# Two attention blocks on one core: row maxima and weighted values turned by VectorE

## The chip, the cores and the metric

The kernel runs on one core of a Trainium2 chip. Times are device microseconds of that core. The engines of the core are named as the profile names them: PE is TensorE's matrix product and PEld its weight load, DVE is VectorE, ACT is ScalarE, POOL is GpSimd and SP is SyncE, which here only issues transfers (DMA). Each engine works its own queue in order. A profile is one execution with every instruction's start and length; the times that are compared are those of several executions without it.

## The reference

Two attention blocks A and B read the same input `x` of 2048 rows and 640 features; a gate mixes their results. Each has 32 heads of 20 features.

```python
qkv = (x @ wqkv).reshape(B, S, 3, H, Dh).transpose(2, 0, 3, 1, 4)
scores = einsum("bhqd,bhkd->bhqk", q, k) * Dh ** -0.5
o = einsum("bhqk,bhkd->bhqd", softmax(scores), v)
attn = o.transpose(0, 2, 1, 3).reshape(B, S, D) @ wo
g = sigmoid((x * gate_w).sum(-1, keepdims=True))
return g * attn_A + (1 - g) * attn_B
```

All inputs and the output are float32. Nothing is masked, so every head has a full 2048 x 2048 matrix of scores.

## The kernel before, in words

The heads are taken four at a time (`GH`), which gives 8 groups for each block and 16 in all. The queries are taken in four blocks of 512 (`QB`). A group with a query block is a unit; there are 64 units. A unit is worked in 8 steps, each with two key tiles of 128 keys, so the main loop has 512 steps.

Each score is computed twice. The first time, in `max_mm`, queries stand on the partitions and 512 keys along the row; only the row's maximum is wanted. Most of these tiles are reduced by VectorE straight from PSUM (line 587). For some, two tiles are combined first: ScalarE keeps the positive part of a difference (line 580) and VectorE adds and takes the maximum in one instruction (line 584). These maxima run up to 15 steps (`LEAD`) ahead of their use. The second time, in `scores`, keys stand on the partitions and 512 queries along the row (line 639). The negated maximum of each query is already in the product, because four extra rows of the query tile `QT` (60 to 63 in each half of 64 partitions) hold it, split into float16 pieces, against rows of a constant in the key tile. ScalarE then takes the exponential out of PSUM (line 642), and `values` multiplies it with the values (line 657). The values have a 21st column of ones, so that each head's 32 rows of the PSUM tile `acc` hold 20 rows of weighted values, then in row 20 (`DH`) the sum of the weights.

Float32 operands of the projections are split into two float16 parts, "high" and "low", and three products are added up. The weighted values are split in the same way before they are stored for the output projection.

Two places are of interest here.

`finish_max` runs when a unit's maxima are complete. `mneg` has 128 queries on the partitions and 16 columns: 4 heads by 4 query tiles. It has to become rows of `QT`, with queries along the row. After a pause, TensorE transposes it (line 600), ScalarE copies and scales the 16x128 result (line 605), GpSimd makes four float16 pieces of it (lines 608 and 610), one transfer writes them to DRAM (line 613), and four transfers read them into `QT` (line 617).

`take_acc` runs when a unit's values are complete. ScalarE copies `acc` to SBUF (line 742), and so frees `acc` for the next unit, which has only this one tile. A transfer collects the four rows of sums as 128x16 (line 748), VectorE takes the reciprocal (line 750), GpSimd splits it into two float16 parts (lines 752 to 754), two transfers lay them out as 8 rows of 512 (line 758), and TensorE spreads these rows over the 32 rows of each head by a product with the constant `sel` (line 763). VectorE multiplies (line 765), GpSimd splits into high and low (lines 768 and 769), and transfers store them (line 774).

The order of all this is fixed while the program is built. A string per step says what comes after what: `e0` and `e1` are score products of the two halves of the partitions, `m0` and `m1` the products for maxima, `V` a values block of eight products, `X` a slot for a piece of a projection:

```python
STEP = ("e0 m1 V e1 m0 e0 m1 e1 m0 e0 m1 e1 m0 V e0 m1 e1 m0",
```

The two other strings have one and three slots `X`, and are taken when projections are due. `finish_max`, `take_acc` and the like are generators in the list `side`. Each `e` advances every one of them by one turn, so a step has 8 turns; `turns(n)` waits n of them. A generator that yields `PRODUCT` is parked until `product()` takes it on, directly ahead of the next `V`. PSUM has `acc` and seven other banks. `take()` picks the bank that a small model of the engines (`clock`, `free_at`, `spend`, `give`, `tick_block`) expects to be free first.

Of the kernel before, what the change touches and what calls it, by code (L numbers as in the profile page):

```python
# [10 lines left out]
F16 = mybir.dt.float16  # L11
F32 = mybir.dt.float32
I32 = mybir.dt.int32
AF = mybir.ActivationFunctionType
OP = mybir.AluOpType
AX = mybir.AxisListType
# [3 lines left out]
P = 128  # L20
# [3 lines left out]
DH = 20  # L24
NT = S // P
NC = D // P
GH = 4
NG = H // GH
GF = GH * DH
QB = 512  # L30
# [5 lines left out]
XE = 7  # L36
QKS = 2.0 ** -12
PARTS = (0, 176, 344, 512)
RS = 2.0 ** 13
OB = 3  # L40
OWAIT = 20
SUM0, SUM1 = -8, 1.9
# [10 lines left out]
T_SCORE, T_MODE, T_VALUES, T_READY = 0.217, 0.1, 0.85, 0.39  # L53
T_EXP, T_MAX, T_BACK = 0.478, 0.6, 0.15
REST = 6
PRODUCT = "product"
ORDER = (0, 2, 1, 3)
LOW = -3.0e38
MS = 2.0 ** 15
# [3 lines left out]
def kernel(  # L63
# [10 lines left out]
    nc = tc.nc  # L74
# [4 lines left out]
    consts = ctx.enter_context(tc.tile_pool(name="consts", bufs=1))  # L79
    wts = ctx.enter_context(tc.tile_pool(name="wts", bufs=2))  # L80
# [4 lines left out]
    ident = consts.tile([P, P], F32, name="ident")  # L85
    make_identity(nc, ident)
    ones = consts.tile([5, P], F32, name="ones")
    nc.vector.memset(ones, 1.0)
    head = consts.tile([2 * GH, GH], F32, name="head")
    nc.gpsimd.tensor_tensor(head, ident[:2 * GH, :GH], ident[:2 * GH, GH:2 * GH], op=OP.add)  # L90
    sel = consts.tile([2 * GH, GH, 32], F16, name="sel")
    nc.vector.tensor_scalar(sel, head.unsqueeze(2).to_broadcast([2 * GH, GH, 32]), 1.0 / RS, None, op0=OP.mult)
    xx = consts.tile([P, 2, NC, S], F16, name="xx")
    xh, xl = xx[:, 0], xx[:, 1]

# [6 lines left out]
    acc = psum.tile([P, QB], F32, name="acc")  # L102
# [15 lines left out]
    clock = {"pe": 0.0, "done": 0.0, "act": 0.0, "dve": 0.0}  # L118
    rows_free = [0.0, 0.0]
    block_end = [0.0, None]  # L120
    free_at, held = [0.0] * NB, set()
    now = [-1]

    def take():

        i = min((k for k in range(NB) if k not in held), key=lambda k: free_at[k])
        held.add(i)
        return i, banks[i]

    def spend(engine, cost, ready=0.0):  # L130

        clock[engine] = max(clock[engine], ready) + cost
        return clock[engine] + T_BACK

    def give(i, t):
        free_at[i] = t
        held.discard(i)
# [7 lines left out]
    def tick_block(cost, ready=0.0):  # L145

        begin = block_end[0] if now[0] < 0 and block_end[1] == rows_free else max(rows_free) + T_MODE
        clock["pe"] = max(begin, ready)
        rows_free[:] = [clock["pe"] + cost + T_MODE] * 2
        block_end[:] = [clock["pe"] + cost, list(rows_free)]  # L150
        clock["done"] = clock["pe"] + cost + T_READY - T_MODE
# [229 lines left out]
    def turns(n):  # L381

        for _ in range(n if now[0] >= 0 else 0):
            yield
# [162 lines left out]
    mparts, ready = {}, set()  # L547
# [42 lines left out]

    def finish_max(g, qb):

        mneg = wts.tile([P, 16], F32, name="mneg", tag="mneg", bufs=2)
        nc.vector.tensor_reduce(mneg, mparts.pop((g, qb)).rearrange("p a b c d -> p (a b c) d"), axis=AX.X,
                                op=OP.max, negate=True)
        for _ in range(REST):
            yield
        yield PRODUCT
        i, pt = take()
        nc.tensor.transpose(pt[:16, :P], mneg, ident)  # L600
        tick_block(0.1, free_at[i])
        yield
        give(i, spend("act", 0.3, clock["done"]))
        mt = wts.tile([16, P], F32, name="mt", tag="mt", bufs=2)
        nc.scalar.activation(mt, pt[:16, :P], AF.Copy, scale=0.5 / MS)  # L605
        m4 = wts.tile([16, 4, P], F16, name="m4r", tag="m4r", bufs=2)
        for k in range(2):
            nc.gpsimd.tensor_copy(m4[:, k, :], mt)  # L608
        for k in range(2):
            nc.gpsimd.tensor_tensor(m4[:, 2 + k, :], mt, m4[:, 0, :], op=OP.subtract)  # L610
        yield from turns(8)
        ms = m_scr[qb % 2]
        nc.sync.dma_start(ms.rearrange("k r q -> r k q"), m4)
        yield from turns(5)
        for h in range(GH):
            base, pair = 60 + 64 * (h % 2), h // 2
            nc.sync.dma_start(QT[g % 2][base:base + 4, pair, qb * QB:(qb + 1) * QB],
                              ms[:, 4 * h:4 * h + 4, :].rearrange("k t q -> k (t q)"))
        ready.add((g, qb))
# [118 lines left out]

    def take_acc(g, qb):

        ot = work.tile([P, QB], F32, name="ot", bufs=2)
        nc.scalar.activation(ot, acc, AF.Copy)  # L742
        spend("act", T_EXP)
        few, many = (2, 8) if g == 2 * NG - 1 else (6, 24)
        sq = work.tile([P, 16], F32, name="sq", bufs=2)
        sh = work.tile([P, 2, 16], F16, name="sh", bufs=2)
        yield from turns(few)
        nc.sync.dma_start(sq, ot.rearrange("(h e) q -> h e q", e=32)[:, DH, :])
        yield from turns(many)
        nc.vector.reciprocal(sq, sq)  # L750
        spend("dve", 0.25)
        nc.gpsimd.tensor_scalar(sq, sq, RS, None, op0=OP.mult)
        nc.gpsimd.tensor_copy(sh[:, 0], sq)
        nc.gpsimd.tensor_tensor(sh[:, 1], sq, sh[:, 0], op=OP.subtract)
        yield from turns(few)
        sr = work.tile([2 * GH, QB], F16, name="sr", bufs=1)
        for k in range(2):
            nc.sync.dma_start(sr[GH * k:GH * k + GH], sh[:, k])
        yield from turns(many)
        yield PRODUCT  # L760
        i, pt = take()
        tick_block(T_SCORE, free_at[i])
        nc.tensor.matmul(pt, sel.rearrange("k h e -> k (h e)"), sr, start=True, stop=True)  # L763
        yield
        nc.vector.tensor_tensor(ot, ot, pt, op=OP.mult)  # L765
        give(i, spend("dve", 0.7, clock["done"]))
        o = work.tile([P, 2, QB], F16, name="on", bufs=2)
        nc.gpsimd.tensor_copy(o[:, 0], ot)  # L768
        nc.gpsimd.tensor_tensor(o[:, 1], ot, o[:, 0], op=OP.subtract)
        if g < 2 * NG - 1:  # L770
            yield from turns(16)
            for h in range(GH):
                f = (g % NG * GH + h) * DH
                nc.sync.dma_start(o_scr[g // NG][:, f:f + DH, qb * QB:(qb + 1) * QB].rearrange("k d q -> d k q"),
                                  o[32 * h:32 * h + DH])
            stored.add((g, qb))
        else:
            last.append((qb, o))
# [9 lines left out]
    def take_last():  # L788

        ot = work.tile([P, QB], F32, name="ot", bufs=2)  # L790
        nc.scalar.activation(ot, acc, AF.Copy)
        i, pt = take()
        one = ident.rearrange("p (h e) -> p h e", e=32)[:, :, DH]
        for t in range(4):
            nc.tensor.matmul(pt[:, 4 * t:4 * t + 4], ot[:, t * P:(t + 1) * P], one, start=True, stop=True)
        rc = work.tile([P, 16], F32, name="sq", bufs=2)
        nc.vector.reciprocal(rc, pt[:, :16])
        give(i, spend("dve", 0.3))
        i, pt = take()
        nc.tensor.transpose(pt[:16, :P], rc, ident)  # L800
        rt = wts.tile([16, P], F32, name="mt", tag="mt", bufs=2)
        nc.scalar.activation(rt, pt[:16, :P], AF.Copy)
        give(i, spend("act", 0.3))
        i, pt = take()
        for t in range(4):
            nc.tensor.matmul(pt[:, t * P:(t + 1) * P], picks[0].rearrange("p k e -> p (k e)")[:, t * P:(t + 1) * P], rt,
                             start=True, stop=True)
        o = work.tile([P, 2, QB], F16, name="on", bufs=2)
        for t in range(4):
            c = slice(t * P, (t + 1) * P)  # L810
            nc.vector.tensor_tensor(ot[:, c], ot[:, c], pt[:, c], op=OP.mult)
            nc.scalar.activation(o[:, 0, c], ot[:, c], AF.Copy)
            nc.gpsimd.tensor_tensor(o[:, 1, c], ot[:, c], o[:, 0, c], op=OP.subtract)
        give(i, spend("dve", 1.2, spend("act", T_EXP)))
        return o
# [30 lines left out]
    start = start_stack.enter_context(tc.tile_pool(name="start", bufs=1))  # L846
# [53 lines left out]
    r, inv = found  # L900
# [4 lines left out]
    for f in drains:  # L905
# [7 lines left out]
                            op=OP.subtract)  # L913
# [70 lines left out]
    work = ctx.enter_context(tc.tile_pool(name="work", bufs=2))  # L984
# [17 lines left out]
    for g in range(2 * NG):  # L1002
        b = g * NQ * NS
        n = g + 1
        if n < 2 * NG:
# [3 lines left out]
            i = g // 4 + 1  # L1009
            if i < 4:  # L1010
                if g % 4 == 0:
                    z, c0 = i // 2, 320 * (i % 2)
                    parts = max_tasks([[(wqkv[z], part * D + c0 + 160 * k) for k in range(2)] for part in range(2)],
                                      lambda m, i=i: scales_qk(i, m))
# [6 lines left out]
            if gg < NG and g % 2 == 0:  # L1021
                load, scale, split = weights_v(gg)
# [4 lines left out]
    for z in range(2):  # L1027
        b = (6, 12)[z] * NQ * NS
        parts = max_tasks([[(wo[z], 160 * k) for k in range(4)]], lambda m, z=z: scales_o(z, m), wrow[z])
        tasks(b + 8, 1, parts)  # L1030
        b = ((NG - 1) * NQ * NS + 4, (NG + 5) * NQ * NS - 4)[z]
# [89 lines left out]
    for G in range(STEPS + 1):  # L1121
        g, qb, i = unit_of(G)
# [12 lines left out]
        for what in (STEP[blocks] if maxima or some else LATE + " X" * (blocks == 2)).split():  # L1135
            k = count[what] = count.get(what, 0) + 1
# [58 lines left out]
```

## Time and profile before

| what | value |
|---|---|
| median of 3 runs | 2867.42 us (2866.15 to 2869.01) |
| profiled execution | 2865.34 us, span 2863.5 us |
| granted TensorE clock | 0.997 |
| busy PE, ACT, DVE, POOL | 98%, 90%, 84%, 24% of the span |
| moved by DMA | 114.77 MB in 176761 packets |

The span runs from the first to the last instruction of the profile. "Busy" counts the time in which an engine had at least one instruction under way; register, semaphore and transfer-issuing instructions do not count. Products are pipelined, so several can be under way at once, and their modelled lengths overlap. The chain of waits is followed back from the last instruction: at each step to what released it, or to the instruction ahead of it on its engine; a line's share of the chain says how much of the span hung on it. In the groups of instructions, `out<-in` are the program's tile names, `x63` is the count, then come busy microseconds, the mean of one in nanoseconds, and the idle time of the engine just before them with what ended it. In the order of time, a row has its start, its length, the engine, the line, the operation, the tiles and the count of merged instructions.

### The profile page before, as it was taken

What the parts mean: (1) busy time and instruction counts of PE and PEld (TensorE: products, weight loads), DVE (VectorE), ACT (ScalarE), POOL (GpSimd) and SP (SyncE); (2) the same over time, 40 slices, a digit from 0 to 9 for tenths busy, and PEclk for the clock granted to TensorE, in tenths of its full rate; (3) what the DMA queues carried; (4) which work ended last, traced back from release to release, by engine and by line L of the source; (5) the groups of instructions that cost most, each with busy time, mean ns of one, the idle gap of its engine ahead of it and who ended that gap; (6) DMA issues with size and microseconds to landing.
All of it is one profiled execution on the core that took longest, in us unless ns stands there. A gap on an engine that the chain in (4) does not pass through costs nothing.

```text
span 2863.5 us, 63124 instructions
## 1 busy us (share of the span) xinstructions
PE 2805.2 (98%) x23489; PEld 982.2 (34%) x23489; DVE 2405.1 (84%) x4637; ACT 2567.4 (90%) x5249; POOL 678.5 (24%) x1103
## 2 busy tenths in 40 slices
PE   6999999999999999999999999999999999999998
PEld 3533223342323323343233333334433333332222
DVE  6688898878898898978988888887788888889982
ACT  3799999989999999989999999998899999888987
POOL 5322113221221212233431111322112233120011
PEclk9999999999999999999999999999999999999999
DMA  4110101001020101202022020210202112221222
GB/s 134 41 38 6 37 10 41 15 15 31 14 52 17 31 15 27 50 10 52 18 45 53 14 60 16 47 37 21 47 21 54 44 35 66 62 72 52 69 61 74
DMA packets 176761, 114.77 MB, mean 40 GB/s; under 512 B 111812, under 2 KB 150396, under 8 KB 176452
## 3 DMA queue, kind: packets, MB, share of 16 engines
q1 hardware_dynamic: 173908, 109.12, 15.9%
q8 instruction: 184, 3.01, 0.4%
q0 software_dynamic: 1600, 0.96, 0.2%
q14 instruction: 125, 1.02, 0.1%
q10 hardware_dynamic: 944, 0.66, 0.1%
HBM read 48.89 MB, written 26.61 MB: 26 GB/s over the span
## 4 chain that ended last, share of the span: by engine, by line
PE 91%; DVE 3%; ACT 2%; DMA 1%; issue 1%; POOL 1%; SPq 0%; POOLq 0%; ACTq 0%; DVEq 0%
PE acc L657 34%; PE bank L639 19%; PE bank L377 19%; PE bank L576 17%; DVE mpart L587 2%; ACT pt L642 1%; PE bank L763 1%; ACT rl L580 1%; PE bank L600 0%; DMA xs<-in_A_x_dram 0%; DMA wv<-in_A_wqkv_dram 0%; DVE rl L584 0%; PE bank L185 0%; ACT ot L742 0%; PE bank L880 0%
## 5 line engine op out<-in xcount | busy, mean ns | idle before, releaser
L642 ACT ACTIVATE pt<-bank 128x512 f32<-128x512 f32 x4096 | 2179.1, 613 | 154.5 <-PE bank L639 85.6
L587 DVE TENSOR_REDUCE mpart<-bank 128x1 f32<-128x512 f32 x2976 | 1883.8, 684 | 337.4 <-PE bank L576 202.8
L657 PE MATMUL acc<-pt,v 128*21 128x512 f32 x8192 | 1081.8, 600 | 2.5 <-ACT ot L742 2.4
L639 PE MATMUL bank<-qt,kt 64*128 64x512 f16 x4096 | 1054.7, 380 | 7.2 <-ACT pt L642 2.9
L576 PE MATMUL bank<-kt,qt 60*128 60x512 f16 x3536 | 1011.0, 380 | 4.6 <-DVE mpart L584 0.9
L576 PEld LDWEIGHTS <-qt 60*128 60x128 f16 x4096 | 235.2, 94 | 679.3 <-issue 621.6
L639 PEld LDWEIGHTS <-kt 64*128 64x128 f16 x4096 | 248.8, 94 | 461.6 <-issue 329.1
L584 DVE CUSTOM_DVE_ANT_0 rl<-bank,rl 128x512 f32<-128x512 f32 x560 | 378.6, 680 | 23.0 <-PE bank L576 9.2
L580 ACT ACTIVATE rl<-bank 128x512 f32<-128x512 f32 x560 | 332.8, 600 | 13.7 <-PE bank L576 11.4
L377 PE MATMUL bank<-xx,wbh 128*128 128x168 f16 (+2 forms) x2240 | 280.0, 244 | 4.5 <-ACT xx L884 1.9
L657 PEld LDWEIGHTS acc<-pt,v 128*21 128x21 f32 x8192 | 143.1, 99 | 403.8 <-issue 384.3
L377 PE MATMUL bank<-xx,wbl 128*128 128x168 f16 (+2 forms) x1120 | 253.0, 243 | 0.0
L768 POOL CAST on<-ot 128x512 f16<-128x512 f32 x63 | 38.5, 611 | 822.6 <-DVE ot L765 796.0
L377 PEld LDWEIGHTS <-wbh 128*128 128x128 f16 x2240 | 184.2, 98 | 87.4 <-issue 80.5
L576 PE MATMUL bank<-kd,qt 60*128 60x512 f16 x560 | 203.5, 381 | 1.6 <-DMA kd<-dd 1.2
L377 PE MATMUL bank<-wvh,xx 128*128 128x160 f16 (+1 forms) x1280 | 155.4, 234 | 0.5 <-ACT rl L580 0.2
L377 PE MATMUL bank<-woh,o_in 128*128 128x160 f16 (+1 forms) x960 | 155.7, 256 | 0.0
L377 PEld LDWEIGHTS <-xx 128*128 128x128 f16 x1920 | 131.9, 97 | 52.2 <-issue 49.0
L377 PE MATMUL bank<-wvl,xx 128*128 128x160 f16 (+1 forms) x640 | 137.3, 231 | 0.6 <-POOL wvl L317 0.6
L608 POOL CAST m4r<-mt 16x128 f16<-16x128 f32 x128 | 33.4, 284 | 437.8 <-ACT mt L605 437.8
L377 PEld LDWEIGHTS <-o_in 128*128 128x128 f16 (+1 forms) x1440 | 104.0, 97 | 75.3 <-issue 62.0
L404 ACT ACTIVATE fs<-bank 128x168 f32<-128x168 f32 (+1 forms) x216 | 69.3, 321 | 52.4 <-PE bank L377 38.7
(137 smaller groups left out, 1395.5 us busy)
## 6 DMA issues: line engine op xcount, KB each, us to landing
y_scr<-y_out SPq DMA_DIRECT2D x32, 320.0 KB
kt<-cq SPq DMA_DIRECT2D x120, 80.0 KB
o_scr<-on SPq DMA_DIRECT2D x240, 40.0 KB
kt<-cq SPq DMA_DIRECT2D x136, 40.0 KB
xs<-in_A_x_dram SPq DMA_DIRECT2D x8, 640.0 KB
o_in<-o_scr SPq DMA_DIRECT2D x32, 160.0 KB
y_out<-y_scr SPq DMA_DIRECT2D x16, 320.0 KB
xx<-y_scr SPq DMA_DIRECT2D x16, 320.0 KB
```

What stands on the lines that cost most here:

```text
L377: nc.tensor.matmul(out_ap, a, b, start=(k == 0), stop=(k == len(pairs) - 1))
L404: nc.scalar.activation(f[:, m], pt[:, m], AF.Copy, scale=QKS)
L576: nc.tensor.matmul(pt, QT[g % 2][r, pair, q0:q0 + P], k, start=True, stop=True)
L580: nc.scalar.activation(relus[u, j], pt, AF.Relu)
L584: nc.vector.tensor_tensor_reduce(rl, pt, rl, 1.0, LOW, OP.add, OP.max, m)
L587: nc.vector.tensor_reduce(m, pt, axis=AX.X, op=OP.max)
L608: nc.gpsimd.tensor_copy(m4[:, k, :], mt)
L639: nc.tensor.matmul(et, KT[g % 2][r, pair, kt * P:(kt + 1) * P], QT[g % 2][r, pair, qb * QB:(qb + 1) * QB], start=True, stop=True)
L642: nc.scalar.activation(pt, et, AF.Exp, scale=factor(g // 4))
L657: nc.tensor.matmul(acc[32 * h:32 * h + VW, :], V[(g // 2) % 2][:, kt, (g % 2) * GH + h, :], ptiles.pop((G, kk, h)), start=(kt == 0), stop= ...
L763: nc.tensor.matmul(pt, sel.rearrange("k h e -> k (h e)"), sr, start=True, stop=True)
L768: nc.gpsimd.tensor_copy(o[:, 0], ot)
```

## The change

VectorE has a transpose that turns each square of 32x32 within a tile by itself. The change uses it in both places.

In `finish_max`, VectorE turns `mneg`, now 128x32 with 16 columns of zeros, in four squares. The result `mt` has the 16 rows of each query tile of 32 queries on partitions 32a to 32a+15. GpSimd scales it and makes the four float16 pieces in three instructions on 128 partitions. There are two turns of waiting instead of the pause, the parked product and ScalarE's copy. Four transfers instead of one write the pieces to DRAM, each for 32 queries of every 128.

In `take_acc`, VectorE turns `acc` out of PSUM in its 64 squares. Then queries stand on the partitions and the features and the sum of each head along the row, so the reciprocal of the sums can be taken in place (128x16) and GpSimd multiplies the whole tile by it with a broadcast. VectorE turns the product back, and the split into high and low follows as before. The copy by ScalarE, the three transfers, the float16 split of the reciprocals, the product with `sel` and VectorE's multiplication are gone. The turns of waiting go from 6 + 24 + 6 + 24 to 6 + 16.

`take_last`, which does the same for the very last unit, keeps TensorE's way; only its tile gets a name of its own.

```diff
-    head = consts.tile([2 * GH, GH], F32, name="head")
-    nc.gpsimd.tensor_tensor(head, ident[:2 * GH, :GH], ident[:2 * GH, GH:2 * GH], op=OP.add)
-    sel = consts.tile([2 * GH, GH, 32], F16, name="sel")
-    nc.vector.tensor_scalar(sel, head.unsqueeze(2).to_broadcast([2 * GH, GH, 32]), 1.0 / RS, None, op0=OP.mult)
+    mnegs = [consts.tile([P, 32], F32, name=f"mneg{i}") for i in range(2)]
+    for t in mnegs:
+        nc.gpsimd.memset(t, 0.0)
...
     def finish_max(g, qb):
 
-        mneg = wts.tile([P, 16], F32, name="mneg", tag="mneg", bufs=2)
-        nc.vector.tensor_reduce(mneg, mparts.pop((g, qb)).rearrange("p a b c d -> p (a b c) d"), axis=AX.X,
+        mneg = mnegs[qb % 2]
+        nc.vector.tensor_reduce(mneg[:, :16], mparts.pop((g, qb)).rearrange("p a b c d -> p (a b c) d"), axis=AX.X,
                                 op=OP.max, negate=True)
-        for _ in range(REST):
-            yield
-        yield PRODUCT
-        i, pt = take()
-        nc.tensor.transpose(pt[:16, :P], mneg, ident)
-        tick_block(0.1, free_at[i])
-        yield
-        give(i, spend("act", 0.3, clock["done"]))
-        mt = wts.tile([16, P], F32, name="mt", tag="mt", bufs=2)
-        nc.scalar.activation(mt, pt[:16, :P], AF.Copy, scale=0.5 / MS)
-        m4 = wts.tile([16, 4, P], F16, name="m4r", tag="m4r", bufs=2)
-        for k in range(2):
-            nc.gpsimd.tensor_copy(m4[:, k, :], mt)
-        for k in range(2):
-            nc.gpsimd.tensor_tensor(m4[:, 2 + k, :], mt, m4[:, 0, :], op=OP.subtract)
+        mt = wts.tile([P, 32], F32, name="mt", tag="mt", bufs=2)
+        nc.vector.transpose(mt, mneg)
+        spend("dve", 0.2)
+        yield from turns(2)
+        nc.gpsimd.tensor_scalar(mt, mt, 0.5 / MS, None, op0=OP.mult)
+        m4 = wts.tile([P, 4, 32], F16, name="m4r", tag="m4r", bufs=2)
+        two = mt.unsqueeze(1).to_broadcast([P, 2, 32])
+        nc.gpsimd.tensor_copy(m4[:, :2], two)
+        nc.gpsimd.tensor_tensor(m4[:, 2:], two, m4[:, :2], op=OP.subtract)
         yield from turns(8)
         ms = m_scr[qb % 2]
-        nc.sync.dma_start(ms.rearrange("k r q -> r k q"), m4)
+        for a in range(4):
+            nc.sync.dma_start(ms[:, :, 32 * a:32 * a + 32].rearrange("k r q -> r k q"), m4[32 * a:32 * a + 16])
...
     def take_acc(g, qb):
 
-        ot = work.tile([P, QB], F32, name="ot", bufs=2)
-        nc.scalar.activation(ot, acc, AF.Copy)
-        spend("act", T_EXP)
-        few, many = (2, 8) if g == 2 * NG - 1 else (6, 24)
+
+        turned = work.tile([P, QB], F32, name="ot", bufs=2)
+        nc.vector.transpose(turned, acc)
+        spend("dve", T_MAX)
+        few, many = (2, 8) if g == 2 * NG - 1 else (6, 16)
         sq = work.tile([P, 16], F32, name="sq", bufs=2)
-        sh = work.tile([P, 2, 16], F16, name="sh", bufs=2)
+        t3 = turned.rearrange("p (b e) -> p b e", e=32)
+        nc.vector.reciprocal(sq, t3[:, :, DH])
+        spend("dve", 0.25)
         yield from turns(few)
-        nc.sync.dma_start(sq, ot.rearrange("(h e) q -> h e q", e=32)[:, DH, :])
+        nc.gpsimd.tensor_tensor(t3, t3, sq.unsqueeze(2).to_broadcast([P, 16, 32]), op=OP.mult)
         yield from turns(many)
-        nc.vector.reciprocal(sq, sq)
-        spend("dve", 0.25)
-        nc.gpsimd.tensor_scalar(sq, sq, RS, None, op0=OP.mult)
-        nc.gpsimd.tensor_copy(sh[:, 0], sq)
-        nc.gpsimd.tensor_tensor(sh[:, 1], sq, sh[:, 0], op=OP.subtract)
-        yield from turns(few)
-        sr = work.tile([2 * GH, QB], F16, name="sr", bufs=1)
-        for k in range(2):
-            nc.sync.dma_start(sr[GH * k:GH * k + GH], sh[:, k])
-        yield from turns(many)
-        yield PRODUCT
-        i, pt = take()
-        tick_block(T_SCORE, free_at[i])
-        nc.tensor.matmul(pt, sel.rearrange("k h e -> k (h e)"), sr, start=True, stop=True)
-        yield
-        nc.vector.tensor_tensor(ot, ot, pt, op=OP.mult)
-        give(i, spend("dve", 0.7, clock["done"]))
+        ot = work.tile([P, QB], F32, name="ob", bufs=1)
+        nc.vector.transpose(ot, turned)
+        spend("dve", T_MAX)
         o = work.tile([P, 2, QB], F16, name="on", bufs=2)
```

More of the change, by code (lines that the diff above doesn't have):

```diff
@@ L38 @@
 PARTS = (0, 176, 344, 512)
-RS = 2.0 ** 13
 OB = 3
@@ L800, in take_last @@
         nc.tensor.transpose(pt[:16, :P], rc, ident)
-        rt = wts.tile([16, P], F32, name="mt", tag="mt", bufs=2)
+        rt = wts.tile([16, P], F32, name="rt", tag="rt", bufs=1)
         nc.scalar.activation(rt, pt[:16, :P], AF.Copy)
```

## The prediction

> **What bounds the kernel now.** I read the page's busy times and chain of waits first, to see which engine the end hangs on; columns are busy microseconds, share of the span, instructions.
>
> ```profile
> PE 2805.2 (98%) x23489; PEld 982.2 (34%) x23489; DVE 2405.1 (84%) x4637; ACT 2567.4 (90%) x5249; POOL 678.5 (24%) x1103
> ...
> PE 91%; DVE 3%; ACT 2%; DMA 1%; issue 1%; POOL 1%; SPq 0%; POOLq 0%; ACTq 0%; DVEq 0%
> ```
>
> TensorE is busy 98% of the span and holds 91% of the chain that ended last. A busy TensorE need not be a full one, so I took the same chain by line, then one stretch in the middle.
>
> ```profile
> by line: PE acc L657 33.8%; PE bank L639 19.0%; PE bank L377 18.8%; PE bank L576 17.2%; DVE mpart L587 2.0%; ACT pt L642 1.4%; issue 1.1%; PE bank L763 0.7%; ACT rl L580 0.5%; PE bank L600 0.5%; DMA xs<-in_A_x_dram 0.5%; DMA wv<-in_A_wqkv_d
> ```
>
> ```profile
> 1000.00:1200.00 200.00, 197.73 (x1547) 57.88 (x1544) 182.48 (x350) 189.99 (x386) 45.08 (x75) 1.00 0.14 31
> ```
>
> The two TensorE products that the change removes, L763 and L600, stand on the chain with 0.7% and 0.5% of 2863.5 us: 20.0 and 14.3 us. But in the second fence (columns: stretch, length, busy PE, PEld, DVE, ACT, POOL) ACT is busy 95% and DVE 91% of the same time: behind the bound stand two engines with little room, and the change moves work onto the second. So the question is how much of the TensorE time comes back as waits for VectorE.
>
> **TensorE: two products go.** Their price is start to start in the order of time, not their modelled length. The first three rows are around an L763, the next two an ordinary step without it, the last three around an L600 and the copy that frees its bank.
>
> ```profile
> 205.66 0.38 PE L576 MATMUL bank<-kt,qt 60*128 60x512 f16 x2
> 205.97 0.39 PE L763 MATMUL bank<-sr,sel 8*128 8x512 f16 x1
> 206.28 1.06 PE L657 MATMUL acc<-pt,v 128*21 128x512 f32 x8
> ...
> 207.72 0.40 PE L639 MATMUL bank<-qt,kt 64*128 64x512 f16 x2
> 208.05 1.06 PE L657 MATMUL acc<-pt,v 128*21 128x512 f32 x8
> ...
> 505.88 0.28 PE L600 MATMUL bank<-ident,mneg 128*16 128x128 f32 x1
> 506.09 1.06 PE L657 MATMUL acc<-pt,v 128*21 128x512 f32 x8
> ...
> 508.10 0.25 ACT L605 ACTIVATE mt<-bank 16x128 f32<-16x128 f32 x1
> ```
>
> From L763 to the values block is 0.31 us, from L600 to it 0.21. The score ahead of L763 starts 0.31 us before it, and in the ordinary step the score starts 0.33 us before the values; so the gap behind a score stays and the product's own slot goes. With 63 and 64 of them (counts in the next fence): 63 x 0.31 = 19.5 us and 64 x 0.21 = 13.4 us, together 32.9, close to the chain's 34.3. I take 32.9. Bounds: 0 if the slots only covered a wait (rival D), 34.3 by the chain.
>
> **VectorE, ScalarE, GpSimd.** Groups by line, with count, busy time and mean ns of one, then idle time ahead:
>
> ```profile
> L769 POOL TENSOR_TENSOR on<-ot,on 128x512 f16<-128x512 f32 x63 | 73.1, 1160 | 5.1
> ...
> L610 POOL TENSOR_TENSOR m4r<-mt,m4r 16x128 f16<-16x128 f32 x128 | 51.5, 419 | 0.0
> ...
> L765 DVE TENSOR_TENSOR ot<-ot,bank 128x512 f32<-128x512 f32 x63 | 42.7, 678 | 0.0
> ...
> L742 ACT ACTIVATE ot<-acc 128x512 f32<-128x512 f32 x63 | 39.0, 619 | 2.0 <-issue 1.2 <-PE acc L657 0.5
> ...
> L608 POOL CAST m4r<-mt 16x128 f16<-16x128 f32 x128 | 33.4, 284 | 437.8 <-ACT mt L605 437.8
> ...
> L763 PE MATMUL bank<-sr,sel 8*128 8x512 f16 x63 | 24.0, 381 | 1.2 <-DMA sr<-sh 0.2
> ...
> L600 PE MATMUL bank<-ident,mneg 128*16 128x128 f32 x64 | 17.7, 277 | 2.1 <-DVE mpart L587 1.0 <-ACT pt L642 0.3
> ...
> L752 POOL TENSOR_SCALAR sq<-sq 128x16 f32<-128x16 f32 x63 | 16.1, 255 | 416.8 <-DVE sq L750 377.8 <-DVE m L271 13.7 <-DMA qt<-rk 9.4
> L605 ACT ACTIVATE mt<-bank 16x128 f32<-16x128 f32 x64 | 16.0, 251 | 0.0
> ...
> L594 DVE TENSOR_REDUCE mneg<-mpart 128x16 f32<-128x64 f32 x64 | 14.0, 219 | 5.7
> ```
>
> The trace has no VectorE transpose. The row nearest to the two large ones (128x512 f32, one out of PSUM, one within SBUF) is L765, 0.678 us for as many columns; I take that. Bounds: 0.63 us, the pace of back-to-back reductions (row further down), and two passes, 1.356 us. The small one (128x32) I price like L594, 0.219; its two passes would add 14 us of VectorE in all. VectorE then gains 126 x 0.678 + 64 x 0.219 = 99.4 us and loses L765's 42.7: net +56.7. The reduction to the maxima and the reciprocal stay.
>
> What of it reaches the end? Today 3% of the span, 86 us of VectorE's 2405.1, lies on the chain: 3.6% of its work. That is the average; after the change VectorE runs at 87% instead of 84%, so an added microsecond costs more than an average one. I take a tenth; bounds are 0, since the two products also cease to hold one of the seven PSUM banks (L600's from 505.88 until its copy ends at 508.35), and a quarter.
>
> ScalarE loses L742 and L605, 55.0 us; at its share of the chain (2% of the span over 2567.4 us, so 2.2%) that is -1.2 us, bounds 0 and twice that.
>
> GpSimd loses L608, L610, L752 and the two other small operations on the reciprocals (priced like L752, 0.255 us each), some 133 us, and gets 63 multiplications like L769 (73 us) and three small operations a unit (0.255, 0.284, 0.419 by the rows, 61 us): +1 us on an engine 76% idle, cost nothing. Were that cover gone, a late multiplication would hold up the second transpose in VectorE's queue and every reduction behind it; it has 16 turns, two steps or some 10 us, to finish.
>
> **The accumulator's wait.** The first transpose takes L742's place, and VectorE's queue is in order: it waits for the unit's last values product, and behind it stand the reductions that free banks, for which TensorE waits. A close case, where the next values block already waits for the copy today, then the row that counts these waits (total, times, longest):
>
> ```profile
> 713.21 1.06 PE L657 MATMUL acc<-pt,v 128*21 128x512 f32 x8
> ...
> 713.37 0.68 DVE L584 CUSTOM_DVE_ANT_0 rl<-bank,rl 128x512 f32<-128x512 f32 x1
> 713.97 0.08 DVE L584 DVE_READ_ACCUMULATOR2_ANT mpart<- 128x1 f32 x1
> ...
> 714.38 0.60 ACT L742 ACTIVATE ot<-acc 128x512 f32<-128x512 f32 x1
> ...
> 715.03 1.06 PE L657 MATMUL acc<-pt,v 128*21 128x512 f32 x8
> ```
>
> ```profile
> PEld acc L657 <- ACT ot L742: 9.0, 13, 1.4
> ```
>
> VectorE is done with the reductions at 714.05, so a transpose would also start at 714.38 and take 0.678 instead of 0.60: the next values start 0.08 us later. VectorE stands idle 0.33 us before it. Over the 13 counted places that is 1.0 us on TensorE and 4.3 us more VectorE time, 61.0 in all. Elsewhere the next block comes later than the copy needs it and nothing is lost.
>
> **DMA queue.** Medians of the issues on SP (min/median/max ns):
>
> ```profile
> L613 SPq DMA_DIRECT2D m_scr<-m4r x64: 308/313/1467, 93.0 to 2788.8; - x64
> ...
> L758 SPq DMA_DIRECT2D sr<-sh x126: 546/584/653, 186.8 to 2820.3; - x126
> ...
> L748 SPq DMA_DIRECT2D sq<-ot x63: 563/593/637, 166.0 to 2814.2; - x63
> ```
>
> A unit issues three more maxima writes (3 x 0.313) and drops one sums read and two spreads (0.593 + 2 x 0.584): 0.82 us less. The maxima reach the queue earlier than now, because the pause for a TensorE place goes. Only the first unit is waited for:
>
> ```profile
> 96.54 0.32 ACT L404 ACTIVATE fs<-bank 128x176 f32<-128x176 f32 x1 [0.81 <-DMA qt<-m_scr]
> ```
>
> That is a gain of 0.8 us at most, left out; later maxima run up to 15 steps ahead. Cost nothing; if a unit's maxima came late, TensorE's next scores would stand.
>
> [...] Back-to-back reductions show what a VectorE operation occupies:
>
> ```profile
> 499.43 1.89 DVE L587 TENSOR_REDUCE mpart<-bank 128x1 f32<-128x512 f32 x3 [0.16 <-PE bank L639]
> ```
>
> Three take 1.89 us, 0.63 each, no more than their own length. [...]
>
> **Sum.** -32.9 (TensorE) + 6.1 (a tenth of 61.0) + 1.0 (accumulator) - 1.2 (ScalarE) = -27.0 us. The profiled execution took 2865.34 us (span 2863.5) and becomes 2838.3; the median of the three runs lies 2.1 above it, 2867.42, and becomes 2840.4. I say 2840. The forecast's own bounds: -34.3 - 2.4 = -36.7 gives 2831; a quarter of VectorE's time, -32.9 + 15.3 + 1.0, gives 2851.
>
> **Rivals.**
>
> B, VectorE becomes the pace. If 40% of its added time is paid, as in a stretch where it is already over 90% busy, the sum is -32.9 + 24.4 + 1.0 - 1.2 = -8.7, so 2859. For it: 91% in the middle stretch. Against: only 2.0% of the chain is L587.
>
> C, slower: a 4-byte transpose takes two passes. Place: the first transpose, between two units, and the queue behind both. A transpose longer by d costs 13d at the close places and adds 126d to VectorE, so with a quarter paid the total is -17.8 + 44.5d; it turns slower from d = 0.40 (a transpose of 1.08 us), and at 1.356 us gives +12, so 2880. For it: no row shows a transpose. Against: every VectorE row of 512 f32 columns here is near 0.68. [...]
>
> D, the slots only covered a wait: both products stand directly ahead of a values block, which needs ScalarE's exponentials. If all were cover, -32.9 goes and +5.9 stays, 2873; if L763 alone, 2860; in the middle 2867, no change. For it: ScalarE's 95%. Against: the ordinary step above has the values 0.33 us behind the score, no wait to cover.
>
> **Chances.** Forecast 0.70, B 0.12, C 0.08, D 0.10. About 0.2%, 5.7 us, is what the measurement can tell from no change. Faster: the forecast, 0.10 of B, 0.03 of D, together 0.83. Same: 0.02 of B, 0.01 of C, 0.04 of D, 0.07. Slower: 0.07 of C, 0.03 of D, 0.10. The range takes in the forecast's bounds and most of B: 2830 to 2858; outside lie C and much of D.
>
> **What would show it.** Right: the values block starts 0.31 us behind a score everywhere; PE's busy time falls by what L763 and L600 had; transposes near 0.68 us; ACT loses 55 us; DVE's share of the chain grows by no more than some 6 us. Wrong: transposes over 1 us (C); waits of PE for mpart grown by 20 us or more (B); values blocks waiting for L642 where the products stood (D).

## The result and the profile after

The changed kernel takes 2834.41 us in the median (2833.04 to 2834.73, 4 runs) against 2866.95 us of the kernel before (2866.15 to 2869.01, 4 runs). The ratio is 0.9884, with a 95% interval of 0.9867 to 0.9902: 1.2% faster, 32.5 us by the medians. The forecast was 2840, with a range of 2830 to 2858.

The page of the changed kernel: busy times, then the chain by engine; below it the chain by line.

```profile
span 2832.8 us, 62443 instructions
...
PE 2773.1 (98%) x23362; PEld 970.8 (34%) x23362; DVE 2443.8 (86%) x4763; ACT 2529.7 (89%) x5122; POOL 671.8 (24%) x914
...
PE 91%; DVE 5%; ACT 1%; DMA 1%; POOL 1%; issue 1%; SPq 0%; POOLq 0%; DVEq 0%; ACTq 0%
```

```profile
by line: PE acc L650 33.6%; PE bank L375 19.5%; PE bank L632 19.0%; PE bank L574 17.5%; DVE mpart L585 3.5%; ACT pt L635 0.8%; issue 0.7%; DVE rl L582 0.7%; DMA xs<-in_A_x_dram 0.5%; ACT rl L578 0.4%; DMA wv<-in_A_wqkv_dram 0.4%; DVE ot L73
```

The span is 30.7 us shorter and TensorE's busy time 32.1 us (2805.2 before). L763 and L600 are off the chain. The lines have moved: L650 is the values block (L657 before), L632 the scores (L639), L585 the reductions (L587), L635 the exponentials (L642). VectorE's reductions went from 2.0% of the chain to 3.5%, that is from 57 to 99 us, although the span fell by nearly what the two products had held.

The groups that the change added on VectorE, and two of those on GpSimd (count, then busy microseconds and mean ns of one):

```profile
L744 POOL TENSOR_TENSOR ot<-ot,sq 128x512 f32<-128x512 f32 x63 | 66.0, 1047 | 993.0 <-DVE sq L741 993.0
...
L736 DVE STREAM_TRANSPOSE ot<-acc 128x512 f32<-128x512 f32 x63 | 44.9, 712 | 5.1 <-PE acc L650 2.7
L747 DVE STREAM_TRANSPOSE ob<-ot 128x512 f32<-128x512 f32 x63 | 44.1, 700 | 0.0
...
L598 POOL TENSOR_SCALAR mt<-mt 128x32 f32<-128x32 f32 x64 | 18.6, 290 | 248.2 <-DVE mt L595 234.0 <-DVE both L186 11.4 <-DMA kd<-dd 2.8
...
L595 DVE STREAM_TRANSPOSE mt<-mneg 128x32 f32<-128x32 f32 x64 | 13.5, 211 | 2.2
```

The transposes take 0.712, 0.700 and 0.211 us; 480 further columns cost 0.49 us, about 1.02 ns each. Rival C had priced 512 columns, in two passes, at 1.356 us. VectorE got 44.9 + 44.1 + 13.5 = 102.5 us and lost L765's 42.7: 59.8 more.

The order of time at a place that answers to the one shown around L763:

```profile
206.34 0.38 PE L574 MATMUL bank<-kt,qt 60*128 60x512 f16 x2
206.65 1.06 PE L650 MATMUL acc<-pt,v 128*21 128x512 f32 x8
```

The values start 0.31 us behind the score, with nothing between. Over all 1024 values blocks of the trace the median is 0.31 us too.

### The profile page after: what moved, and what is told of

The parts are those of the page before. It is cut to its first block, busy times and chain, and to the rows that moved or that the text cites. A ratio compares the mean times of both kernels' runs of the same rounds, so it can differ in the third digit from the quotient of the medians.

```text
span 2832.8 us, 62443 instructions
## 1 busy us (share of the span) xinstructions
PE 2773.1 (98%) x23362; PEld 970.8 (34%) x23362; DVE 2443.8 (86%) x4763; ACT 2529.7 (89%) x5122; POOL 671.8 (24%) x914
## 4 chain that ended last, share of the span: by engine, by line
PE 91%; DVE 5%; ACT 1%; DMA 1%; POOL 1%; issue 1%; SPq 0%; POOLq 0%; DVEq 0%; ACTq 0%
PE acc L650 34%; PE bank L375 20%; PE bank L632 19%; PE bank L574 17%; DVE mpart L585 3%; ACT pt L635 1%; DVE rl L582 1%; DMA xs<-in_A_x_dram 0%; ACT rl L578 0%; DMA wv<-in_A_wqkv_dram 0%; DVE ot L736 0%; PE bank L813 0%; PE bank L183 0%; PE bank L862 0%; DVE wmax L227 0%
## 5 line engine op out<-in xcount | busy, mean ns | idle before, releaser
L635 ACT ACTIVATE pt<-bank 128x512 f32<-128x512 f32 x4096 | 2157.5, 614 | 155.0 <-PE bank L632 75.1
L585 DVE TENSOR_REDUCE mpart<-bank 128x1 f32<-128x512 f32 x2976 | 1867.8, 681 | 264.3 <-PE bank L574 167.1
L650 PE MATMUL acc<-pt,v 128*21 128x512 f32 x8192 | 1082.0, 600 | 3.4 <-DVE ot L736 3.1
L632 PE MATMUL bank<-qt,kt 64*128 64x512 f16 x4096 | 1056.3, 380 | 11.9 <-ACT pt L635 4.5
L632 PEld LDWEIGHTS <-kt 64*128 64x128 f16 x4096 | 248.1, 94 | 456.7 <-issue 322.8
L578 ACT ACTIVATE rl<-bank 128x512 f32<-128x512 f32 x560 | 329.8, 595 | 14.6 <-PE bank L574 12.3
L744 POOL TENSOR_TENSOR ot<-ot,sq 128x512 f32<-128x512 f32 x63 | 66.0, 1047 | 993.0 <-DVE sq L741 993.0
L650 PEld LDWEIGHTS acc<-pt,v 128*21 128x21 f32 x8192 | 143.0, 99 | 434.6 <-issue 421.5
L404 POOL CAST cq<-fs 128x512 f16<-128x512 f32 x60 | 36.6, 609 | 446.0 <-ACT fs L402 444.0
```

The costliest lines, as they stand in the source:

```text
L404: nc.gpsimd.tensor_copy(hi, f)
L578: nc.scalar.activation(relus[u, j], pt, AF.Relu)
L585: nc.vector.tensor_reduce(m, pt, axis=AX.X, op=OP.max)
L632: nc.tensor.matmul(et, KT[g % 2][r, pair, kt * P:(kt + 1) * P], QT[g % 2][r, pair, qb * QB:(qb + 1) * QB], start=True, stop=True)
L635: nc.scalar.activation(pt, et, AF.Exp, scale=factor(g // 4))
L650: nc.tensor.matmul(acc[32 * h:32 * h + VW, :], V[(g // 2) % 2][:, kt, (g % 2) * GH + h, :], ptiles.pop((G, kk, h)), start=(kt == 0), stop= ...
```

## The experiments

Each was timed beside the kernel before on the same chip. The kernel before was at 2866.12 us in the first set, 2865.74 in the second and 2867.11 in the third; the changed kernel, run again in the first two, at 2834.69 and 2834.53.

**The changed kernel again**, twice, as the base.

> The changed kernel once more, as the base for the others of this set. Every theory: 32.5 us below the kernel before, as measured (2834.4 against 2867.0).

> The changed kernel again, as the base of this set. Every theory expects the 2834.4 to 2834.7 us that it took before.

Ratios 0.989 (0.9875 to 0.9905) and 0.9892 (0.9877 to 0.9907). In these two sets the runs of this kernel lie between 2834.26 and 2835.46, so a microsecond or two between kernels of a set can be seen in the medians, though not in the intervals of the ratios, which carry the scatter of the kernel before. In the third set the changed kernel was not run again, and the kernel before took 1.0 and 1.4 us more than in the other two; differences from the changed kernel there can be too large by about that.

**The maxima alone.** `finish_max` as changed, `take_acc` as before:

```diff
 # in the kernel before
-        i, pt = take()
-        nc.tensor.transpose(pt[:16, :P], mneg, ident)
...
+        nc.vector.transpose(mt, mneg)
...
```

> The kernel before with only the maxima turned by VectorE; the weighted values keep their transfers and the TensorE product. Theory of the slots (a product taken off TensorE gives its start-to-start slot, whatever VectorE gets for it): 64 x 0.21 = 13.4 us, so 2853.5. The forecast's tenth of VectorE's added 14 us would take 1.4 back: 2855. Rival, the product only covered a wait for exponentials: no change, 2867. Theory that the gain comes from the values' part alone: 2867 too.

2851.50 us, ratio 0.9949 (0.9936 to 0.9963): 14.6 us faster than before, a little more than the slots of L600.

**The values alone.** `take_acc` as changed, `finish_max` as before:

```diff
 # in the changed kernel
-        nc.vector.transpose(mt, mneg)
...
+        nc.tensor.transpose(pt[:16, :P], mneg, ident)
...
```

> The changed kernel with the maxima going through TensorE and ScalarE as before; only the weighted values are turned by VectorE. Theory of the slots: 63 x 0.31 = 19.5 us, so 2847.5, and with the maxima-only run's gain the whole 32.5. The forecast's tenth of VectorE's 43 us and the accumulator's 1 us would leave -14.3: 2852.6. If VectorE's time were paid to 40%: -2, 2865.

2849.71 us, ratio 0.9942 (0.9928 to 0.9955): 16.4 us faster than before, 3.1 less than L763's slots. The two parts add up to 31.0 of the 31.4 us of the whole in the same set, so the total can be looked at in these two parts.

**The product back, without a reader.**

```diff
+    idle_w = consts.tile([8, P], F16, name="idle_w")
+    idle_x = consts.tile([8, QB], F16, name="idle_x")
...
         yield from turns(many)
+        yield PRODUCT
+        i, pt = take()
+        tick_block(T_SCORE, free_at[i])
+        nc.tensor.matmul(pt, idle_w, idle_x, start=True, stop=True)
+        yield
+        give(i, clock["done"])
         ot = work.tile([P, QB], F32, name="ob", bufs=1)
```

> The changed kernel with one idle product of 8 rows by 512 columns, whose result nobody reads, put back ahead of a values block in each unit: only the TensorE slot returns, with no reader on VectorE and no transfer. Theory of the slots: 63 x 0.31 = 19.5 us more than the changed kernel, 2854. Rival, the slot covers a wait: the same time as the changed kernel, 2834. If the gain came from the dropped transfers and the freed bank: nearly 2834 as well.

2851.12 us, ratio 0.9946 (0.9933 to 0.996): 16.4 us over the changed kernel. Neither a reader nor a transfer came back with the slot. A bank did, for one turn, and the second transpose comes later than in the changed kernel, so these are part of the 16.4. It is 3.1 less than the start-to-start time of 19.5. Rival D, that the slots were all cover, falls for L763.

**One more transpose.**

```diff
-        yield from turns(many)
+        for _ in range(1):
+            yield from turns(many // 1)
+            spare = work.tile([P, QB], F32, name="spare", bufs=1)
+            nc.vector.transpose(spare, turned)
+            spend("dve", T_MAX)
         ot = work.tile([P, QB], F32, name="ob", bufs=1)
```

> The changed kernel with one further transpose of 128x512 per unit on VectorE, into a tile that nobody reads: 63 x 0.70 = 44 us more VectorE time. Theory that VectorE's time is covered by TensorE: 0 to +1 us. The forecast's tenth: +4.4 us, 2839. Rival B's 40%: +18 us, 2852.

2848.75 us, ratio 0.9941 (0.9928 to 0.9955): 14.2 us over the changed kernel. Its groups and its chain by line:

```profile
L748 DVE STREAM_TRANSPOSE spare<-ot 128x512 f32<-128x512 f32 x63 | 44.2, 702 | 0.0
```

```profile
by line: PE acc L650 32.8%; PE bank L375 19.5%; PE bank L632 18.3%; PE bank L574 17.1%; DVE mpart L585 4.2%; ACT pt L635 1.2%; issue 0.7%; DVE rl L582 0.7%; ACT rl L578 0.6%; DMA xs<-in_A_x_dram 0.5%; DMA wv<-in_A_wqkv_dram 0.4%; DVE ot L73
```

The reductions' share of the chain rises from 3.5% to 4.2%, about 20 us. 44.2 us of VectorE cost 14.2 us of time: 32%. As the price of an added operation my tenth falls, and so does the theory that TensorE covers VectorE. Of rival B this was the price, nearly.

**Four more transposes**, the same loop with `range(4)` and `turns(many // 4)`.

> The same with four further transposes per unit, spread over the turns of waiting: 176 us more VectorE time, some 2620 us in all or 92% of the span. Covered: under +3 us. A tenth: +18 us, 2852. 40%: +70 us, 2905. A price that rises with the load: clearly more than four times that of the run with one.

2892.94 us, ratio 1.0097 (1.0082 to 1.0113): 58.4 us over the changed kernel, 14.6 for each. The price does not rise with the load in this range; it is a third from the first to the fourth. This is also how the change would have turned slower: at three such operations a unit more than it has (43 us), the gain of 32 is gone.

**One more, far from the others.** In one_more the added transpose stands directly ahead of the second one, so the two form a block of 1.4 us. Here it stands alone, and works on tiles that are always ready:

```diff
+    spares = [consts.tile([P, QB], F32, name=f"spare{i}") for i in range(2)]
...
             stored.add((g, qb))
+            yield from turns(6)
+            nc.vector.transpose(spares[1], spares[0])
+            spend("dve", T_MAX)
```

> The changed kernel with one idle transpose of 128x512 per unit on VectorE (44 us more), on tiles that are always ready, and about 22 turns behind the second transpose instead of directly ahead of it. Theory of the backlog (VectorE's queue and the seven banks absorb one operation of 0.7 us, and what costs is a second one before the first is worked off): under +5 us, 2839. Theory that VectorE's time costs a third wherever it stands: +14 us, 2849, as in the run with one more beside the other.

2849.18 us, ratio 0.9938 (0.9924 to 0.9951), 14.7 us over the changed kernel's 2834.5 of the other sets. The added line stands in a branch that the last units do not take, so there are 60 of these transposes and not 63, 42.1 us in all; the price is 35% of that. An added transpose costs about as much alone as beside another. The theory of the backlog, which I had formed after the first set, falls.

If 59.8 us more VectorE time is paid to a third, the change should have lost 19 us of the 33 that TensorE gave. It did not. Either something else gave back about as much, or the change's own operations cost less than the added ones. Two runs looked for the first.

**ScalarE's copy back, idle.**

```diff
+    spares = [consts.tile([P, QB], F32, name=f"spare{i}") for i in range(2)]
...
         nc.vector.transpose(turned, acc)
         spend("dve", T_MAX)
+        nc.scalar.activation(spares[1], spares[0], AF.Copy)
+        spend("act", T_EXP)
```

> The changed kernel with ScalarE's copy back in each unit at its old place, but on two spare tiles that are always ready, so that it takes ScalarE's time (63 x 0.62 = 39 us) and nobody waits for it. The forecast's price by the share of the chain: +0.9 us, 2835.5. Rival, ScalarE's relief is what paid for VectorE's added time: +5 us or more, 2840. Paid to a third, as VectorE's time in the run with one more transpose: +13, 2847.

2836.25 us, ratio 0.9893 (0.9878 to 0.9908): 1.7 us over the changed kernel of the other sets. All its runs (2836.09 to 2836.73) lie above all of that base, but by the ratios, 0.9893 against 0.989 and 0.9892, less than 1 us is left. It is small either way.

```profile
L741 ACT ACTIVATE spare<-spare 128x512 f32<-128x512 f32 x63 | 41.6, 661 | 0.0
```

41.6 us of ScalarE cost some 4%, against VectorE's 32%, although ScalarE is busy for the larger part of the span (89% against 86%). ScalarE's relief is not what paid.

**One bank out of use.** Nothing is added to any engine; the builder keeps a bank for four turns, and the second transpose comes those turns later.

```diff
         yield from turns(many)
+        i, _ = take()
+        yield from turns(4)
+        give(i, free_at[i])
         ot = work.tile([P, QB], F32, name="ob", bufs=1)
```

> The changed kernel with one of the seven PSUM banks kept out of use for four turns (about 2.8 us) per unit ahead of the second transpose, as the removed product and its multiplication held one: nothing else is added. The forecast's lower bound named the freed bank as a relief. If it is worth something: +2 to +5 us, 2837 to 2840. If six banks do for so long: 0 to +1 us, 2835.

2849.34 us, ratio 0.9941 (0.9927 to 0.9954): 14.8 us over the changed kernel. Its chain by line has no line that could be called the cause:

```profile
by line: PE acc L650 33.6%; PE bank L375 19.5%; PE bank L632 18.9%; PE bank L574 17.3%; DVE mpart L585 3.2%; ACT pt L635 1.6%; issue 0.7%; DVE rl L582 0.6%; DMA xs<-in_A_x_dram 0.5%; ACT rl L578 0.5%; DMA wv<-in_A_wqkv_dram 0.4%; DVE ot L73
```

Four turns are half a step, 2.8 us (2832.8 us over 512 steps). In the kernel before, L763 held its bank for 3.1 us in the place shown, from 205.97 to L765's end at 209.09, and for 2.7 us on average of the 63 (1.6 to 3.7). So a bank out of use for so long, once in a unit, costs as much here as one more transpose. The run also delays the second transpose, but the loss stands ahead of that: 14.9 us of it fall between the two values blocks where the bank is taken. Whether the price goes by the length of the hold was not varied, nor was a bank taken at L763's own place; the last part of this section comes back to that.

**The accumulator copied by ScalarE first.**

```diff
-        nc.vector.transpose(turned, acc)
+        plain = work.tile([P, QB], F32, name="ob", bufs=1)
+        nc.scalar.activation(plain, acc, AF.Copy)
+        spend("act", T_EXP)
+        nc.vector.transpose(turned, plain)
         spend("dve", T_MAX)
```

> The changed kernel with the accumulator copied to SBUF by ScalarE as before (0.62 us, 39 us in all) and VectorE turning the copy: gives back ScalarE's time and frees the accumulator by ScalarE's queue. If the accumulator's wait on VectorE costs (24 places wait 13.7 us after, 18 places 11.5 us before): up to 2 us faster, 2832. If ScalarE's time costs its share of the chain: +1 us, 2835. If ScalarE's relief was a large part of the gain: over +5 us, 2840.

2888.11 us, ratio 1.0078 (1.0064 to 1.0091): 53.6 us over the changed kernel, slower than the kernel before, and none of the expectations. From its waits (total, times, longest):

```profile
DVE ot L739 <- ACT ob L737: 61.3, 61, 4.2
...
PE bank L574 <- DVE mpart L585: 23.4, 39, 0.8
```

VectorE's transpose now stands in its queue until ScalarE has got through its own queue to the copy, about 1 us in each of 61 units; the reductions behind it free no banks meanwhile, and TensorE waits for them: 23.4 us in the row above, 0.7 in the changed kernel. In the traces, the stretch from a unit's last values block to the next unit's first is 45.0 us longer in all. The same ScalarE time without a waiter cost 1.7 us in scalar_back, so it is the wait, not the copy. The prediction named this danger for the first transpose; in the changed kernel it does not arise, because there the transpose waits only for the values block itself (idle 5.1 us before it in all, 2.7 of them on that block, in the row of L736 above).

**A later first values block.**

```diff
+FIRST = "e0 m1 e1 m0 e0 m1 V e1 m0 e0 m1 e1 m0 V e0 m1 e1 m0"
...
-        for what in (STEP[blocks] if maxima or some else LATE + " X" * (blocks == 2)).split():
+        for what in ((FIRST if G % NS == 1 and not blocks else STEP[blocks]) if maxima or some else LATE + " X" * (blocks == 2)).split():
```

> The changed kernel with the first values block of a unit two pairs of score and maximum products later in its step, where no projection is due (the order of the first step string alone changes, in the second step of a unit): the accumulator has 0.4 us longer to be turned. The places that wait for it are 24 with 13.7 us in the changed kernel. If these waits end on the path: 6 to 12 us faster, 2823 to 2829. If the wait only moves to a bank: no change, 2834.5.

2834.22 us, ratio 0.9885 (0.987 to 0.99): no change. Who waited for the first transpose, in the changed kernel:

```profile
L736 DVE STREAM_TRANSPOSE ot<-acc x63: 701/716/718, 163.5 to 2780.8; 128x512 f32<-128x512 f32 x63
...
who waited for it (us, times):
  PEld acc L650: 10.6, 14
  PE acc L650: 3.1, 10
```

The same answer for this run:

```profile
L737 DVE STREAM_TRANSPOSE ot<-acc x63: 706/716/718, 163.5 to 2781.0; 128x512 f32<-128x512 f32 x63
...
who waited for it (us, times):
busy tenths in 40 slices 0000000000000000000000000000000000000000
```

Nobody waited for it any more, and the time is the same. Taking this wait away gained nothing; whether it comes back elsewhere or the changed order costs as much was not tested. No version that was run beats the changed kernel by more than its runs scatter.

**Where in a unit the time goes.** A unit has 16 values blocks, numbered 0 to 15 here, and every trace has the starts of all of them. For two kernels, I take the time from each values block to the next and add up the difference over the units, without the first; a stretch of four such times is a quarter of a unit. In the changed kernel, the first large transpose starts behind block 15, the second in most units behind block 4 or 5. In the kernel before, L600 stands in most units behind block 2, L763 behind 13 or 14, and L765 behind 14 or 15. Microseconds in all:

| difference | from 0 to 4 | 4 to 8 | 8 to 12 | 12 to the next unit | sum |
|---|---|---|---|---|---|
| changed kernel again, less changed kernel | 0.1 | 0.1 | 0.0 | 0.0 | 0.2 |
| kernel before, less values alone | -0.8 | -5.2 | 0.1 | 22.6 | 16.8 |
| values alone, less changed kernel | 15.1 | 0.3 | 0.0 | -0.2 | 15.2 |
| product back, less changed kernel | 1.0 | 17.2 | 0.0 | -0.1 | 18.0 |
| one more, less changed kernel | 0.7 | 13.5 | 0.5 | 0.1 | 14.8 |
| one apart, less changed kernel | 0.0 | 0.0 | 13.9 | 1.2 | 15.1 |
| bank held, less changed kernel | 0.0 | 15.2 | 0.5 | -0.2 | 15.5 |

Each difference stays within the quarter where something was changed, or just behind it; the third quarter, where the change has nothing, shows 0.1. The second row is the change of the values alone: it gave 22.6 us where the product, its multiplication and their bank had been, and lost 6.0 us in the two quarters where the transposes stand in place of ScalarE's copy and the transfers. That is 7% of the transposes' 89.0 us, far below the third that an added one costs.

## Why the prediction was right, and where it was not

**What bounds.** Right. TensorE's slots made most of the gain: 22.6 and 15.1 us at the places of L763 and L600, whose slots are 19.5 and 13.4.

**TensorE, -32.9.** Right in sign and nearly in size. The slot of L763, put back, cost 16.4 us instead of 19.5. In that trace the time from the values block ahead of the product to the next is 18.9 us longer in all, and the two times behind it are 3.2 shorter; why they are shorter was not tested. L600's slot was not put back by itself.

**VectorE's durations.** Right: 0.712, 0.700 and 0.211 us against 0.678, 0.678 and 0.219. Rival C, with its 1.356 us, falls.

**A tenth of VectorE's time, +6.1.** Its reason was wrong. Runs with one and four more transposes, beside another or far away, all paid about a third. I had taken the share of the chain, 3.6%, and trebled it. The share says where the chain ran, not what a microsecond costs: in the changed kernel it rose by 42 us for the reductions while the span fell. For the change itself the size was nearly right: its two large transposes cost 6.0 us at their places, where the forecast's tenth of 89.0 us and the accumulator's 1.0 make 9.9. With the reason gone, that is luck. Why the same operation costs a third when it is added and 7% in the change stays open.

**The freed banks, used only as a bound of 0 for VectorE's price.** The run with a bank held invites a tidy account, in which VectorE's time cost a third and the bank paid for it: -16.4 (slot) + 46.3 x 0.32 = +14.8 (two transposes less L765), -1.7 (ScalarE) and -14.8 (bank) make -18.1, and -16.4 was measured for the values alone. But two of its terms cancel, and place by place it does not hold. By these prices L763's place would have given 16.4 + 14.8 + 13.7 (L765's 42.7 us at 0.32) = 44.9 us, and it gave 22.6; the transposes would have cost 28.5, and cost 6.0. So beyond the slot some 6 us are left for L765's time and the bank together, and how they share them was not tested. For the maxima, -13.4 + 13.5 x 0.32 = +4.3 and -0.7 for ScalarE (its 16.0 us at 4%) make -9.8, and -14.6 was measured. The 4.8 us left over can be the bank that L600 held, its weight load, which had waited 23.9 us in all for reductions, or the same too high price; no run tells them apart.

**The sum.** The forecast was 27.0 us and 32.5 were measured. By place, the transposes cost some 4 us less than forecast and the maxima gave some 3 more, while L763's place gave some 2 less than its slot, a tenth of L765 and ScalarE's copy. The errors are small, and partly cancel.

**ScalarE, -1.2.** Right in size, as far as can be told: 41.6 us of it cost 1.7 or less in scalar_back, so 55.0 us are 2.3 or less. Its busy time fell by 37.7 us, though, not by the 55 that was named as a sign; why was not looked into.

**The accumulator, +1.0.** As a wait it came as forecast: values blocks' weight loads waited 10.6 us at 14 places after, against 9.0 us at 13 before. late_values, which took the wait away, was no faster.

**GpSimd and the queues, 0.** Nothing contradicts it: GpSimd's busy time went from 678.5 to 671.8 us. The 256 writes of maxima were not varied on their own.

**Rivals.** B had nearly the right price for an added microsecond of VectorE, 40% against a measured third, but not for the change's own. Its sign, waits of TensorE for the maxima's reductions grown by 20 us or more, did not come: these waits went from 2.4 to 3.8 us. That alone would not refute it, since they are 4.5 us in the run with one more transpose, which is 14.2 us slower. D fell with product_back. Three back-to-back reductions took 1.89 us in the kernel before, less than three times their mean of 0.684, so no gap stood behind one of them. The trace with one more transpose shows none between two transposes:

```profile
180.91 0.70 DVE L748 STREAM_TRANSPOSE spare<-ot 128x512 f32<-128x512 f32 x1
181.54 0.67 DVE L751 STREAM_TRANSPOSE ob<-ot 128x512 f32<-128x512 f32 x1
```

The second transpose starts 0.63 us behind the first, less than the first one's own 0.70, and so at all 63 places.

## What to carry to other kernels

Price an added microsecond on a second engine by adding an idle operation and timing it, not by that engine's share of the chain: here VectorE at 86% cost about a third, ScalarE at 89% some 4%. But such a price holds for that addition. Added up, the prices of a slot, a bank and a multiplication came to twice what their place gave, and the change's own transposes cost a fifth of theirs. So compare the two traces stretch by stretch as well, and see where the time went, before a sum of prices is believed because its total fits. And look out for an operation that must wait for another busy engine's queue: where ScalarE copied the accumulator first, it held up the reductions behind it on its own engine, and 1 us of such a wait in each unit cost 53.6 us, against 14.2 for 0.7 us of work.

## What was not expected of the hardware

The price of added VectorE time is even: 14.2 us for 44.2, 14.7 for 42.1 and 58.4 for 176.2, from 86% to 89% busy and at each place that was tried. That ScalarE, busier by the page, costs an eighth of it or less was not foreseen, and why was not tested. Nor was it foreseen that one of seven banks out of use for 2.8 us in each unit costs 14.8 us in all.
